# One attention head's exponentials and values left unsplit in float32, and new costs in the list schedule's model

## The chip, the cores and the metric

The kernel runs on one core of one Trainium2 chip. The metric is the device time of one execution in microseconds (us), as a median of several runs. A core has five engines that run beside each other: TensorE (PE), VectorE (DVE), ScalarE (ACT), GpSimd (POOL) and SyncE (SP), which here issues the transfers.

## The reference

A masked attention feeds two gated feed-forward stages. All arrays are float64 or float32; seq is 768, 2 x 8 heads of 64.

```python
q_bits = (einsum('bhsd,dk->bhsk', q, proj) > 0)      # 6 hash bits
mask = q_bucket[:, :, :, None] == k_bucket[:, :, None, :]
scores = where(mask, scale * q @ k.T, -1e9)
attn = exp(scores - max(scores));  attn /= sum(attn) + 1e-9
x = (attn @ v)                      # [1536, 512]
h = ((x @ w1) * (x @ w2)) @ w3;  x = h @ w_out          # 1024 wide
out = (1/(1+exp(-(x @ w_gate))) * (x @ w_val)) @ w_out2 # 1536 wide
```

## The kernel before

The weights arrive as 64-bit floats. Each tile st of 128 x 512 of them is loaded by SP (line 412) and decoded in six steps by ACT, POOL and DVE (`decode`, lines 428 to 437; their tiles are da and dr). A product at near float32 precision is made in the fast form of PE (float32r): each operand is split into a high part, a copy rounded to float32r, and a low part, the rest, and the partial products are added.

Attention goes through 16 heads in groups g of 128 queries, six groups to a head. For each group: four score products into one of two PSUM tiles s (`emit_qk`, lines 558 and 561), the maximum on DVE (sm, line 567), the exponential on ACT (e, line 577), twelve transposes for each two groups on PE (tp, line 612), their copy to the high part pt on ACT (line 615) and the low part on DVE (line 617), and for each two groups the product with the values (av, line 630), from which ACT copies and DVE adds into xall (lines 642 and 643). A head is prepared some groups ahead (`prep`): POOL scales and splits q and k (aq, bq; lines 495 to 497), SP moves parts of them, PE makes the hash bits (gps, lines 479 and 482, with ACT's sg between, line 481), and DVE the mask rows ft (line 504). The values are loaded (line 450) and split (spv, lines 466 and 467) per head. After every second head the row sums go through DRAM to a broadcast tile rr (line 595), and POOL scales xall by it (`emit_scale`, line 602). Between the attention work PE multiplies w3 and w_out into one matrix (wacc, line 685), from the decoded tiles w3f and wor, split into t and wo (lines 672 to 680). From about 340 us on only the feed-forward products are left (line 794), and PE does them one after another.

The order of instructions on each engine does not come from the program text alone. `order_engines` takes all instructions with their dependences, replays them in a list schedule with a table of costs (`cost`, `step`, and the costs of a transfer in `plan`), and tries 6000 random changes of priorities, each kept if the replayed end is not later. The order that is left is fixed as dependences on every engine, SP with its transfers among them. A changed cost can therefore move any instruction.

`PLAIN` is the number of heads, from the first, whose exponentials and values are not split: then there is one pt tile in float32, no low part, no split of the values, and one product per chunk, of 64 instead of 128 rows out.

Of the kernel before, what the change touches and what calls it, by code (L numbers as in the profile page):

```python
# [20 lines left out]
ALU = mybir.AluOpType  # L21
# [30 lines left out]
def order_engines(tc):  # L52
# [5 lines left out]
    ins = [i for i in nc.cur_bb.bb.instructions if type(i).__name__ not in ("BassTilePoolBoundary", "InstRegisterMove")]  # L58
# [3 lines left out]
    N = len(ins)  # L62
# [20 lines left out]
    def cost(k):  # L83

        i, e, op = ins[k], eng[k], type(ins[k]).__name__
        rd = [x for x in i.ins if hasattr(x, "ap")]
        n = max([count(i.outs[0])] + [count(x) for x in rd[:1]])
        bank = lambda x: (region(x) or ("",))[0] in rings and rings[region(x)[0]][0][0] in BANKS
        banks = any(map(bank, rd + [i.outs[0]]))
        es = mybir.dt.size(i.outs[0].dtype)  # L90
        if op.startswith("InstDMA"):
            return 500
        if e == "PE":
            passes = 1 if "float32r" in str(rd[0].dtype) else 2 if n == 128 else 4
            return n / 2.4 * passes + (14 if n == 512 else 16 if passes == 1 else 2 if passes == 2 else 4)
        if e == "Activation":
            if banks:
                return {768: 878, 512: 478, 256: 405}.get(n, 470)
            return 40 + n + (96 if es == 2 else 0)
        if e == "Pool":  # L100
            port[k] = True
            if op == "InstTensorTensor":
                return 30 + n * (2.35 if n < 768 else 2.8)
            return 140 if n < 128 else 715 if es == 2 else 560 if n > 384 else 450
        if e == "DVE":
            two = op in ("InstTensorTensor", "InstCustomDveAnt") or (op == "InstTensorScalarPtr" and len(rd) > 1 and count(rd[1]) > 8)
            if op == "InstTensorReduce":
                return 867
            port[k] = not banks and n >= 128
            if two and n >= 512:  # L110
                return 600
            if two:
                return 85 + n * 1.17 if banks else 60 + n * 1.1
            return 589 if banks else 60 + n * 0.55
        return 500

# [54 lines left out]
    costs = [cost(k) for k in range(N)]  # L171
    left0 = [len(deps[k]) + len(starts[k]) for k in range(N)]
    loads = [type(i).__name__.startswith("InstDMA") for i in ins]

    HORIZON, STRIDE = 30000.0, 15000.0

# [14 lines left out]
    def plan(prio, state, limit):  # L191


        (left, pools, todo, slots, taken, events, ready, waiting, at, free, lock, seen, begun, order,
         tick, dma, slow, window, used, spill) = map(saved, state)
        marks, mark = [], events[0][0] + STRIDE
        pe_order = order["PE"]

        def blocked(k):
            for t in opens.get(k, ()):  # L200
                g = rings[t][0]
                if slots[g] <= 0 or queue[g][taken[g]] != t:
                    return g
                if pools.get(AFTER.get(g[0])):
                    return AFTER[g[0]]
            return None

        def wake(g):
            for k in waiting.pop(g, ()):
                heapq.heappush(ready[eng[k]], (prio[k], k))  # L210

        while events:
            now = events[0][0]
            if now >= mark:
                marks.append((now, [saved(x) for x in (left, pools, todo, slots, taken, events, ready, waiting, at, free, lock, seen,
                                                       begun, order, tick, dma, slow, window, used, spill)]))
                mark = now + STRIDE
            while events and events[0][0] <= now:
                _, _, what, x = heapq.heappop(events)
                if what == "ready":  # L220
                    seen[x] = now
                    heapq.heappush(ready[eng[x]], (prio[x], x))
                elif what == "slot":
                    g = rings[x][0]
                    slots[g] += 1
                    pools[g[0]] -= 1
                    wake(g)
                    if not pools[g[0]]:
                        wake(g[0])
                elif what == "end":  # L230
                    for u in ends[x]:
                        left[u] -= 1
                        at[u] = max(at[u], now + 1.25 * step.get((eng[x], eng[u]), 60))
                        if not left[u]:
                            tick += 1
                            heapq.heappush(events, (at[u], tick, "ready", u))
                    for t in held.get(x, ()):
                        todo[t] -= 1
                        if not todo[t]:
                            tick += 1  # L240
                            heapq.heappush(events, (now + 200, tick, "slot", t))
            again = True
            while again:
                again = False
                for e in ranks:
                    while free[e] <= now and ready[e]:
                        _, k = heapq.heappop(ready[e])
                        g = blocked(k)
                        if g is not None:
                            waiting.setdefault(g, []).append(k)  # L250
                            continue
                        for t in opens.get(k, ()):
                            g = rings[t][0]
                            slots[g] -= 1
                            taken[g] += 1
                            if slots[g] > 0 and waiting.get(g):
                                wake(g)
                                again = True
                        order[e].append(k)
                        begun[k] = now  # L260
                        for u in begins[k]:
                            left[u] -= 1
                            at[u] = max(at[u], now)
                            if not left[u]:
                                tick += 1
                                heapq.heappush(events, (at[u], tick, "ready", u))
                        begin, c = now, costs[k]
                        if e == "PE":
                            if limit and len(pe_order) == limit[0] and now >= limit[1]:
                                return None  # L270
                            while (window + 1) * WINDOW <= now:
                                share, window, used = used / WINDOW, window + 1, spill
                                spill = 0.0
                                slow = share <= 0.75 if slow else share < 0.45
                            c *= 2 if slow else 1
                            inside = min(c, (window + 1) * WINDOW - now)
                            used, spill = used + inside, spill + c - inside
                        if port[k]:
                            begin = max(now, lock["Pool" if e == "DVE" else "DVE"])
                            lock[e] = begin + c  # L280
                        free[e] = done = begin + c
                        if loads[k]:
                            n = count(ins[k].outs[0]) * list(ins[k].outs[0].ap)[0][1] * mybir.dt.size(ins[k].outs[0].dtype)
                            dma = max(now + 2900, dma) + n / 300
                            done = dma + 900
                        tick += 2
                        heapq.heappush(events, (done, tick - 1, "end", k))
                        heapq.heappush(events, (free[e], tick, "free", k))
        if sum(map(len, order.values())) != N:
            return None  # L290
        return max(free.values()), order, seen, begun, marks
# [29 lines left out]
def lsh_attention_moe_moe2_kernel(  # L321
# [115 lines left out]
        dve.tensor_tensor(out=dst.bitcast(I32), in0=ai, in1=ri, op=ALU.add)  # L437


    PLAIN = 0  # L440

    raws, splits, mats = {}, {}, {}

# [153 lines left out]
    def emit_scale(h):  # L597
        b, hh = divmod(h, H)
        x = xall[:, hh // 2, b * S:(b + 1) * S].rearrange("p (c q) -> p c q", c=NT)
        r = rr_t.pop(h // 2).rearrange("p (q c) -> p c q", c=NT)  # L600
        for t in range(0, NT, 2):
            pool.tensor_tensor(out=x[:, t:t + 2], in0=x[:, t:t + 2], in1=r[:, t:t + 2], op=ALU.mult)

    def emit_T(g, j):

# [638 lines left out]
```

## Time and profile before

| | us |
|---|---|
| median of 3 runs | 766.4 (766.24 to 767.06) |
| profiled execution | 769.23 |
| its span, first to last instruction | 767.4 |
| PE busy | 746.2 (97%) |
| DVE busy | 626.3 (82%) |
| ACT busy | 525.3 (68%) |
| POOL busy | 431.4 (56%) |

The profile's page divides the span into 40 slices of some 19 us. PE is busy for half of the first, eight to nine tenths of the next two, and nine tenths or more in nearly all others; DVE and ACT are near full only in the first half. A line of the timeline names an engine, the source line, the operation and the tiles (out<-in); in brackets stands the idle time ahead of it and what ended it. A matmul's shown time is longer than its distance to the next one, because matmuls overlap; the distances are what the chain of waits shows.

### The profile page before, as it was taken

The page shows a single profiled execution, that of the slowest core. Times are in us where ns is not written, and L with a number is a line of the kernel's source. Part 1 is how long each engine was busy: PE and PEld are TensorE (multiplying, and loading weights), DVE is VectorE, ACT ScalarE, POOL GpSimd, SP SyncE. Part 2 cuts the span into 40 slices and gives each one's busy share as a digit, 9 for nine tenths or more (in the row PEclk, how much of TensorE's full clock was granted, in tenths as well). Part 3 has the DMA queues.
Part 4 walks back from the last instruction along what each step waited for, and adds up shares of the span by engine and source line. Part 5 has one row for each costly group of instructions (what it writes and reads, how often), then busy time and mean ns, then how long its engine had stood idle before and what let it go on. Part 6 is the DMA issues. An engine that isn't in the chain of part 4 may idle for free.

```text
span 767.4 us, 11480 instructions
## 1 busy us (share of the span) xinstructions
PE 746.2 (97%) x3896; PEld 638.3 (83%) x3896; DVE 626.3 (82%) x970; ACT 525.3 (68%) x986; POOL 431.4 (56%) x475
## 2 busy tenths in 40 slices
PE   5898999999999999999999999999999999999997
PEld 4787889888989889988888888888888888888886
DVE  6996988776899789869999998788789787676743
ACT  7897988877899889777555568865746444442353
POOL 7767787865577574446655544797654433442000
PEclk9999999999999999999999999999999999999999
DMA  9975767533457755200111143432100000000011
GB/s 289 231 175 149 193 175 205 140 100 115 151 148 168 176 141 142 87 12 1 54 40 45 56 164 124 151 125 97 55 0 28 28 1 1 1 0 2 1 55 56
DMA packets 28506, 74.46 MB, mean 97 GB/s; under 512 B 6048, under 2 KB 8352, under 8 KB 28448
## 3 DMA queue, kind: packets, MB, share of 16 engines
q1 hardware_dynamic: 28368, 73.73, 33.1%
q8 instruction: 31, 0.51, 0.3%
q14 instruction: 27, 0.22, 0.1%
q10 hardware_dynamic: 80, 0.00, 0.0%
HBM read 52.82 MB, written 3.19 MB: 73 GB/s over the span
## 4 chain that ended last, share of the span: by engine, by line
PE 81%; ACT 7%; DVE 5%; POOL 4%; issue 2%; DMA 2%; SPq 0%; DVEq 0%; ACTq 0%; POOLq 0%
PE pa L794 18%; PE pb L794 15%; PE m L794 11%; PE av L630 6%; PE wacc L685 5%; PE tp L612 5%; PE p L794 4%; PE npa L794 4%; PE npb L794 4%; PE s L558 3%; PE s L561 3%; ACT e L577 2%; PE y L794 2%; ACT pt L615 2%; PE gps L479 2%
## 5 line engine op out<-in xcount | busy, mean ns | idle before, releaser
L617 DVE TENSOR_TENSOR pt<-tp,pt 128x512 fp32r<-128x512 f32 x144 | 95.0, 683 | 9.0 <-ACT pt L615 8.1
L612 PE MATMUL tp<-idf,e 128*128 128x128 f32 x576 | 100.3, 276 | 1.8 <-DVE xall L643 0.8
L567 DVE TENSOR_REDUCE sm<-s 128x1 f32<-128x768 f32 x96 | 90.2, 948 | 11.3 <-PE s L561 11.0
L577 ACT ACTIVATE e<-s,sm 128x768 f32<-128x768 f32 x96 | 86.9, 906 | 8.1 <-DVE sm L567 7.6
L431 POOL TENSOR_SCALAR da<-da 128x512 f32<-128x512 f32 x76 | 52.4, 689 | 66.1 <-ACT da L428 59.0
L615 ACT ACTIVATE pt<-tp 128x512 fp32r<-128x512 f32 x144 | 82.4, 599 | 8.6 <-PE tp L612 7.2
L612 PEld LDWEIGHTS tp<-idf,e 128*128 128x128 f32 x576 | 72.0, 141 | 11.6 <-DVE xall L643 2.0
L630 PE MATMUL av<-pt,spv 128*128 128x256 f32 x576 | 79.2, 286 | 0.7 <-DVE ft L504 0.3
L630 PEld LDWEIGHTS av<-pt,spv 128*128 128x128 f32 x576 | 73.2, 190 | 3.6 <-DVE pt L617 1.8
L430 POOL TENSOR_SCALAR dr<-st 128x512 bf16<-128x512 f32 x76 | 67.3, 887 | 6.9 <-issue 1.1
L558 PE MATMUL s<-bk,bq 128*128 128x384 f32 x192 | 62.2, 377 | 6.1 <-ACT e L577 5.4
L561 PE MATMUL s<-ak,aq 128*128 128x384 f32 x192 | 60.8, 376 | 0.0
L429 ACT ACTIVATE dr<-st 128x512 int16<-128x512 uint32 x76 | 60.1, 791 | 0.0
L685 PE MATMUL wacc<-wo,t 128*128 128x512 f32 x192 | 59.3, 407 | 0.0
L428 ACT ACTIVATE da<-st 128x512 f32<-128x512 f32 x76 | 51.1, 672 | 12.0 <-DVE xall L437 3.7
L432 DVE TENSOR_SCALAR da<-da 128x512 uint32<-128x512 uint32 x76 | 47.3, 625 | 9.8 <-POOL da L431 9.8
L558 PEld LDWEIGHTS s<-bk,bq 128*128 128x128 f32 x192 | 36.0, 195 | 11.8 <-ACT e L577 7.8
L794 PE MATMUL pa<-xsx,swh 128*128 128x512 f32 x136 | 42.5, 390 | 0.2 <-DVE w2r L957 0.2
L920 POOL TENSOR_TENSOR swl<-w2r,swh 128x512 fp32r<-128x512 f32 x16 | 21.0, 1313 | 31.2 <-ACT swh L367 28.9
L561 PEld LDWEIGHTS s<-ak,aq 128*128 128x128 f32 x192 | 36.6, 195 | 1.8 <-DVE ak L544 0.3
L685 PEld LDWEIGHTS wacc<-wo,t 128*128 128x128 f32 x192 | 34.3, 189 | 4.2 <-ACT t L367 0.2
L794 PE MATMUL m<-wtl,gh 128*128 128x512 f32 x96 | 37.2, 389 | 0.0
(338 smaller groups left out, 2187.3 us busy)
## 6 DMA issues: line engine op xcount, KB each, us to landing
st<-in_moe_w_dram SPq DMA_DIRECT2D x32, 512.0 KB, 5.2
st<-in_moe_w_out_dram SPq DMA_DIRECT2D x20, 512.0 KB, 3.3
st<-in_moe_w_gate_dram SPq DMA_DIRECT2D x12, 512.0 KB, 3.3
st<-in_moe_w_val_dram SPq DMA_DIRECT2D x12, 512.0 KB, 3.2
qk<-in_qk_dram SPq DMA_DIRECT2D x15, 384.0 KB, 4.3
rawv<-in_v_dram SPq DMA_DIRECT2D x16, 192.0 KB, 2.4
rr<-row SPq DMA_DIRECT2D x16, 192.0 KB, 5.0
out_dram<-o SPq DMA_DIRECT2D x12, 256.0 KB, 2.0
```

Of the source, the lines that this page charges most:

```text
L429: act.activation(out=r.bitcast(I16)[:, 0::2], in_=lw, func=AF.Copy, scale=2.0 ** -29)
L430: pool.tensor_scalar(out=r.bitcast(BF16)[:, 1::2], in0=f(hw), scalar1=0.0, scalar2=1.0, op0=ALU.mult, op1=ALU.mult)
L558: pe.matmul(s[:, half, :HS], lhsT=m["bq"][:, qs], rhs=m["bk"][:, ks], start=True, stop=False)
L561: pe.matmul(s[:, half, :HS], lhsT=m["aq"][:, qs], rhs=m["ak"][:, ks], start=False, stop=True)
L567: dve.tensor_reduce(out=b, in_=s[:, :, :HS], op=ALU.max, axis=AX.XY, negate=True)
L577: act.activation(out=e.rearrange("p (a c) -> p a c", a=2), in_=s[:, :, :HS], func=AF.Exp, bias=sm, scale=1.0, accum_out=su_t[h][:, t:t + 1],)
L612: pe.transpose(ps[:, i * P:(i + 1) * P], e_t[g - g % 2 + a][:, c * P:(c + 1) * P], idf)
L615: act.activation(out=dh, in_=src, func=AF.Copy)
L617: dve.tensor_tensor(out=d, in0=src, in1=f(dh), op=ALU.subtract)
L630: pe.matmul(acc[:w.shape[1], :2 * P].rearrange("p (a t) -> p a t", a=2), lhsT=w, rhs=r[:, :, c], start=(c == 0 and i == 0), stop=(c == NT ...
L685: pe.matmul(acc, lhsT=t3[x][:, j], rhs=wo[y][:, j], start=(j == 0 and n == 0), stop=(j == NF1 - 1 and n == 2))
L794: mm = pe.matmul(ps, lhsT=lhs[x], rhs=rhs[y], start=start and n == 0, stop=stop and n == 2)
```

## The change

PLAIN goes from 0 to 1. The scaling by rr is done in two steps of three chunks instead of three steps of two. In the list schedule's model an ACT step of 256 columns from PSUM costs 290 instead of 405 ns, a DVE step of two operands from PSUM 1.0 instead of 1.17 ns a column, and a transfer's time depends on its kind: loads of 64-bit data, transfers out of on-chip or scratch tiles and other loads have their own rates, and the broadcast read of the row sums a longer tail.

```diff
-                return {768: 878, 512: 478, 256: 405}.get(n, 470)
+                return {768: 878, 512: 478, 256: 290}.get(n, 470)
...
-                return 85 + n * 1.17 if banks else 60 + n * 1.1
+                return 85 + n * 1.0 if banks else 60 + n * 1.1
...
     loads = [type(i).__name__.startswith("InstDMA") for i in ins]
+    wide = [mybir.dt.size(i.outs[0].dtype) == 8 for i in ins]
+    local = [[r[0] for r in map(region, i.ins) if r] for i in ins]
+    rate = [250 if wide[k] else 205 if local[k] else 340 for k in range(N)]
+    slack = [3000 if any(t.startswith("row") for t in local[k]) else 1000 for k in range(N)]
...
-                            dma = max(now + 2900, dma) + n / 300
-                            done = dma + 900
+                            dma = max(now + 1700, dma) + max(300, n / rate[k])
+                            done = dma + slack[k]
...
-    PLAIN = 0
+    PLAIN = 1
...
-        for t in range(0, NT, 2):
-            pool.tensor_tensor(out=x[:, t:t + 2], in0=x[:, t:t + 2], in1=r[:, t:t + 2], op=ALU.mult)
+        for t in range(0, NT, NT // 2):
+            pool.tensor_tensor(out=x[:, t:t + NT // 2], in0=x[:, t:t + NT // 2], in1=r[:, t:t + NT // 2], op=ALU.mult)
```

The source lines after the model move down by four: line 602 before is line 606 after.

The order changes on all engines. Three places matter here; the number behind a name's underline only tells tiles apart, the digits before it are the head or group. First SP's queue at the start, before and after: qk are the heads' queries and keys, rawv and spv values, st weight tiles.

```order
L525 DMA qk00_100<-in_qk_dram 128x384 x2
L527 DMA qk01_101<-in_qk_dram 64x768 x2
L457 DMA qk1_109<-in_qk_dram 128x768
L450 DMA rawv0_111<-in_v_dram 128x384
L457 DMA qk2_143<-in_qk_dram 128x768
L412 DMA st_448<-in_moe_w3_dram 128x512
```

```order
L531 DMA qk01_101<-in_qk_dram 64x768 x2
L461 DMA qk1_109<-in_qk_dram 128x768
L454 DMA spv0_111<-in_v_dram 128x384
L461 DMA qk2_143<-in_qk_dram 128x768
L454 DMA rawv1_167<-in_v_dram 128x384
L416 DMA st_419<-in_moe_w3_dram 128x512
```

Head 0's values go to their final tile, and head 1's values are read ahead of the first weight tile.

Then POOL's queue at the first scaling by rr, before and after: aq4 and bq4 are head 4's operands, one row for each half; da, dr and wo belong to decoding and splitting weights.

```order
L466 CAST spv3_903<-rawv3_532 128x6x64
L467 TENSOR_TENSOR spv3_903<-rawv3_532,spv3_903 128x6x64
L602 TENSOR_TENSOR xall_79<-xall_79,rr0_306 128x256 x3
L496 CAST aq4_776<-qk4_381 128x384
L497 TENSOR_TENSOR bq4_777<-qk4_381,aq4_776 128x384
L588 TENSOR_SCALAR su2_612<-su2_612 128x6
```

```order
L435 TENSOR_SCALAR da_1025<-da_1025 128x512
L434 TENSOR_SCALAR dr_1026<-st_834 128x512
L500 CAST aq4_739<-qk4_361 128x384
L501 TENSOR_TENSOR bq4_740<-qk4_361,aq4_739 128x384
L500 CAST aq4_739<-qk4_361 128x384
L606 TENSOR_TENSOR xall_79<-xall_79,rr0_297 128x384 x2
L501 TENSOR_TENSOR bq4_740<-qk4_361,aq4_739 128x384
```

The scaling moved from ahead of both halves of head 4 to between them (before, the second half's aq and bq follow the rows shown for the first).

Last ACT's queue between the exponentials of groups 17 and 18, before and after.

```order
L577 ACTIVATE e17_804,su2_612<-s1_85,sm17_802 128x768
L367 ACTIVATE xall_79<-av6_827 64x256
L429 ACTIVATE dr_981<-st_790 128x512
L481 ACTIVATE sg_853<-gps_849,zb_78 128x384
L615 ACTIVATE pt0_14_761<-tp15_820 128x512
L367 ACTIVATE wo0_92<-wor4_444 128x512
L481 ACTIVATE sg_861<-gps_857,zb_78 128x384
L428 ACTIVATE da_1062<-st_871 128x512
L615 ACTIVATE pt0_16_888<-tp16_890 128x512
L429 ACTIVATE dr_1063<-st_871 128x512
L615 ACTIVATE pt0_16_888<-tp17_910 128x512
L577 ACTIVATE e18_886,su3_885<-s0_84,sm18_883 128x768
```

```order
L581 ACTIVATE e17_767,su2_576<-s1_85,sm17_765 128x768
L485 ACTIVATE sg_816<-gps_812,zb_78 128x384
L371 ACTIVATE wo0_92<-wor5_416 128x512
L432 ACTIVATE da_1105<-st_909 128x512
L619 ACTIVATE pt0_16_851<-tp16_853 128x512
L581 ACTIVATE e18_849,su3_848<-s0_84,sm18_846 128x768
```

Of the ten steps between the two, four are left; the others now stand before exponential 17, or, as the second sg, behind exponential 18.

## Rows read from the trace of the kernel before

**Rows 1.** Windows: span, busy us of PE, PEld, DVE, ACT, POOL, PE clock, DMA, GB/s

```profile
12.00:20.00 8.00, 4.93 (x28) 3.96 (x28) 5.01 (x9) 7.66 (x16) 7.52 (x10) 1.00 1.01 293
20.00:25.00 5.00, 4.50 (x21) 4.02 (x22) 4.49 (x8) 3.75 (x9) 3.41 (x6) 0.66 1.04 223
...
46.00:58.00 12.00, 12.00 (x85) 10.88 (x84) 11.84 (x20) 11.85 (x26) 5.99 (x9) 1.00 0.94 223
...
62.20:66.00 3.80, 3.80 (x14) 3.72 (x15) 0.00 (x0) 1.54 (x3) 3.56 (x5) 0.55 0.32 74
...
100.00:340.00 240.00, 237.83 (x1511) 214.14 (x1510) 201.40 (x313) 202.69 (x401) 155.04 (x194) 1.00 0.52 141
340.00:768.00 428.00, 423.16 (x1862) 348.68 (x1860) 338.82 (x509) 236.05 (x414) 202.01 (x182) 1.00 0.14 49
```

**Rows 2.** Timeline 58 to 71 us: start us, us, engine, line, operation [idle before, releaser]

```profile
58.36 0.91 ACT L577 ACTIVATE e<-s,sm 128x768 f32<-128x768 f32 x1
58.53 3.11 POOL L602 TENSOR_TENSOR xall<-xall,rr 128x256 f32<-128x256 f32 x3 [2.52 <-DMA rr<-row]
...
62.14 0.68 PE L479 MATMUL gps<-aq,pq 128*128 128x384 f32 x1 [3.12 <-POOL aq L496]
...
64.46 0.58 ACT L481 ACTIVATE sg<-gps,zb 128x384 fp32r<-128x384 f32 x1 [4.03 <-PE gps L479]
...
69.77 0.91 ACT L577 ACTIVATE e<-s,sm 128x768 f32<-128x768 f32 x1
...
70.02 1.67 PE L630 MATMUL av<-pt,spv 128*128 128x256 f32 x12
```

**Rows 3.** Timeline up to 51 us, SP's queue, ACT, DVE and PE

```profile
4.46 0.91 SPq L412 DMA_DIRECT2D st<-in_moe_w_dram  x2
...
8.29 0.55 DVE L466 CAST spv<-rawv 128x384 fp32r<-128x384 f32 x1 [0.64 <-DMA rawv<-in_v_dram]
...
10.56 0.67 ACT L428 ACTIVATE da<-st 128x512 f32<-128x512 f32 x1 [0.40 <-DMA st<-in_moe_w_dram]
...
18.57 0.68 DVE L617 TENSOR_TENSOR pt<-tp,pt 128x512 fp32r<-128x512 f32 x1
...
20.50 0.44 PE L558 MATMUL s<-bk,bq 128*128 128x384 f32 x1 [2.19 <-ACT e L577]
...
50.70 0.86 SPq L595 DMA_DIRECT2D rr<-row  x1
```

**Rows 4.** Chain of waits, 0 to 100 us: start us, us, engine, work

```profile
23.26 0.21 PE tp L612
...
24.76 1.43 PE av L630 x12
...
94.34 0.44 PE tp L612 x4
...
95.34 0.18 PE s L558
...
96.20 0.47 PE wacc L685 x2
```

**Rows 5.** Groups of ACT instructions, 11 to 70 us: count, busy us, mean ns

```profile
L615 ACT ACTIVATE pt<-tp 128x512 fp32r<-128x512 f32 x26 | 15.1, 600 | 1.6 <-PE tp L612 1.3
L429 ACT ACTIVATE dr<-st 128x512 int16<-128x512 uint32 x9 | 7.1, 790 | 0.0
L428 ACT ACTIVATE da<-st 128x512 f32<-128x512 f32 x9 | 6.1, 674 | 0.4 <-DMA st<-in_moe_w_dram 0.4
L481 ACT ACTIVATE sg<-gps,zb 128x384 fp32r<-128x384 f32 x8 | 4.6, 580 | 5.0 <-PE gps L479 5.0
...
L367 ACT ACTIVATE wo<-wor 128x512 fp32r<-128x512 f32 x5 | 3.2, 635 | 0.0
L367 ACT ACTIVATE xall<-av 64x256 f32<-64x256 f32 x7 | 2.7, 380 | 0.6 <-PE av L630 0.5
```

**Rows 6.** Instructions on the tile rr: count, min/median/max ns, first and last start

```profile
L602 POOL TENSOR_TENSOR xall<-xall,rr x24: 857/877/1312, 58.5 to 339.7; 128x256 f32<-128x256 f32 x24
```

## The prediction

> **What bounds the kernel now.** I read the windows first [rows 1]. From 340 us to the end PE is busy for 423.2 us of the 427.4 that the span still has, and from 100 to 340 for 237.8 of 240: there PE alone sets the time, and the change puts no work there. What can move is the first 100 us. In 46 to 58 us PE, ACT and DVE are all nearly full (12.00, 11.85 and 11.84 of 12), so I took the timeline next, to see which of them is waited for. It shows one hole [rows 2]. POOL stands idle for 2.52 us until the read of the row sums (rr) has landed, scales xall for 3.11 us, and only then casts head 4's aq; PE waits 3.12 us for that cast, ACT 4.03 us for the product after it, and the next exponential (number 18, counted from 0) starts at 69.77, 11.4 us after number 17 at 58.36. Right behind the hole, in 62.2 to 66.0 us, the granted clock is 0.55, which is mostly the 1.2 GHz level [rows 1]: 3.80 x 0.45 = 1.7 us of PE more. The hole therefore costs 3.1 + 1.7 = 4.8 us of PE. An earlier, smaller one is PE's wait of 2.19 us for an exponential, before 20.50 us [rows 3], and a clock of 0.66 in the 5 us behind it, 1.7 us more [rows 1]. So ACT's order up to exponential 18, and POOL's order at the scaling, are where the change is decided.
>
> **The change part by part.** I work against the profiled execution: 769.2 us, a span of 767.4 and 1.8 around it. The three timed runs lie at 766.2 to 767.1, median 766.4, so I carry the difference that I find over to 766.4.
>
> *Head 0 unsplit.* Nine subtractions of pt leave DVE, 9 x 0.68 = 6.1 us [rows 3], with three additions into xall behind them. ACT copies as often as before (nine tp tiles, three products), so ACT loses nothing. On PE 36 products of 256 columns become 18. Twelve take 1.43 us, 0.12 each [rows 4], 36 so 4.3 us. No row shows a plain float32 product. Lower bound: each costs what a float32r one does, 18 x 0.12 = 2.1, a gain of 2.1 us. Upper bound: the kernel's split form makes four partial products in two instructions of twice the width, so an unsplit one of 64 columns may need four passes, 18 x 4 x 0.12 = 8.6 us, a loss of 4.3. Transposes lie between: they read float32 too, and 128 columns take 0.11 (four in 0.44), at the low clock 0.21; 256 columns are then 0.22 to 0.42, from -0.3 to +3.3 us in all [rows 4]. I take the upper end, +4.3 us of PE work, since a product needs all partial products and a transpose none. The Trainium skill ("FP8 and Floating Point Precision", TensorE Precision Notes) says that true float32 makes four passes through the array; at 2.4 GHz that is an estimate of 0.43 us for each and +3.4 us in the sum, a rule that speaks against this edit wherever PE has no idle time.
>
> What hides it: the three products fall between about 24 and 43 us, where ACT is the engine that is waited for, and behind the first of them ACT has an exponential and a copy of wo in its queue (the order has both ahead of the xall copy that waits for PE). If that cover is gone, each of the three lengthens the chain by (8.6 - 4.3)/3 = 1.4 us.
>
> *The relieved DVE* is worth little by itself for the same reason. I credit 0.5 us of the 1.25 us that ACT idles in 20 to 25 us [rows 1]; the ends are 0 and 1.25.
>
> *The first loads.* The read of head 1's values now stands ahead of the first two weight tiles on SP. ACT waited 0.40 us for the first of these, started at 10.56, and exponential 0 stands right behind that step in ACT's order [rows 3]. 192 KB at the 293 GB/s of 12 to 20 us [rows 1] are 0.67 us. So the start is 0.6 us later; the bounds are 0 and 0.91, the time SP itself takes to issue two such tiles [rows 3]. The DVE cast of values, which waited 0.64 us for its load, now reads head 1's, which is issued later; it stands between gps and the first maximum, and I take it as covered by the same 0.6.
>
> *ACT's order up to exponential 17.* By count, between exponentials 0 and 17 ACT now has one pt copy, one da, two dr, one wo and one xall more: 0.60 + 0.67 + 2 x 0.79 + 0.64 + 0.38 = 3.9 us [rows 5], that is, more of the weights decoded by then. Exponential 17 starts at 58.4 + 0.6 + 3.9 - 0.5 = 62.4 us, later than before.
>
> *The scaling moved.* In POOL's order the aq and bq of half 0 and the aq of half 1 of head 4 now come ahead of the scaling, and only bq of half 1 behind it. PE's wait of 3.12 us for aq therefore goes. What is late next is that last bq. The read of rr was issued at 50.70 and POOL used it at 58.53 [rows 2, 3], 7.8 us; the new order issues one weight tile ahead of it, and ACT by then runs some 2 us later, so I expect it to land at 60 to 61 us. Two scalings of 384 columns are 2 x 1.5 x 0.88 = 2.6 us (the ends are 2.6 and 3.9, by the 0.86 to 1.31 us of 256 columns [rows 6]) and bq some 1 us: ready at about 64 to 65. PE comes to that product only behind scores that need exponential 17, which ends at 63.3, and ACT's sg stands behind exponential 18. So no wait, or a short one.
>
> *From there to PE's end.* Between the starts of exponentials 17 and 18 ACT has the exponential itself, one sg, one wo, one da and one pt: 0.91 + 0.58 + 0.64 + 0.67 + 0.60 = 3.4 us [rows 2, 5]. Exponential 18 starts at 65.8 instead of 69.77, 4.0 us earlier, at equal ACT work (one da and one wo more, one pt and one sg fewer). On PE, the product av of groups 14 and 15 started at 70.02 [rows 2]. Now it stands behind four score products that need the end of exponential 18, 66.7, with four transposes and two wacc: 4 x 0.18 + 0.44 + 0.47 = 1.6 us [rows 4], so 68.3, 1.7 us earlier. By count of the order PE has then done four score products and three wacc more, 4 x 0.18 + 3 x 0.23 = 1.4 us. In all PE is 1.7 + 1.4 = **3.1 us** ahead, and since PE is nearly full from 100 us on, this stays to the end.
>
> *The rest.* The other scalings, three steps to two at each of eight places, lie on POOL, which is busy 155 of 240 us. The other new costs only move instructions between 80 and 340 us; PE idles there 2.2 us from 100 on [rows 1], so at most 2.2 is to be gained, and a new hole like the old one may cost 4.8. I take 0.
>
> Sum: 769.2 - 3.1 = 766.1 for the profiled execution, 766.4 - 3.1 = **763.3 us** for the median.
>
> **The rivals.**
> 1. *More is won.* The 4.8 us of the hole go wholly, and with DVE out of the way ACT brings exponential 2 forward (in the order it now stands ahead of two pt copies), so that the wait of 2.19 us before 20.50 goes as well. For it: DVE was full in 46 to 58. Against it: ACT was as full. 766.4 - 4.8 - 2.2 = 759.4 us.
> 2. *Nothing comes of it.* ACT's extra 3.9 us cost as much as the hole gave, because the decoded weights only wait, and PE is not ahead. Against it: wacc products did move forward in PE's order. 766.4 - 3.1 + 2.5 to 3.5, about 766.3 us.
> 3. *Slower: the hole moves into the second half.* If rr lands after about 63 us, bq of half 1 is not ready when PE comes to it, and everything behind it on PE stands: the scores of the next groups, hence ACT. The price is a wait like the old one, so the 4.8 us are not saved, and then the late start (0.6) and the float32 work that finds no idle time (up to 2 x 1.4 for the two later av) remain: 766.4 + 3.4 = 769.8 us. For it: rr took 7.8 us here, and a tile of 512 KB now goes ahead of it. With the page's four passes the float32 part would be 2 x 1.1 and the time 769.2.
>
> **How the numbers follow.** Forecast 0.45, rival 1 0.20, rival 2 0.20, rival 3 0.15. A difference of 0.2% (1.5 us) is about what a measurement of this kernel can tell from none; so faster is under 764.9, slower over 767.9. The forecast's own range is 761.5 to 765.5; most of it (0.40 of 0.45) is faster, and all of rival 1; from rival 2 come 0.06 more. Faster 0.66, same 0.20, slower 0.14. The range from 758.0 to 768.3 takes in rivals 1 and 2 and the bounds of the late start and of the DVE relief, and leaves out most of rival 3.
>
> **What would show it.** Right: no PE wait over 1 us between 55 and 70 us, a granted clock of 1.00 there, exponential 18 near 66 us, and PE reaching its last stretch about 3 us earlier. The six float32 products of a pair should take near 2.9 us, without an ACT wait for xall behind them over 1 us. The first weight step on ACT should start near 11.2. Wrong: a wait of PE on bq of head 4, a new wait of more than 2 us between 80 and 340, or a start that is late by more than 1 us.

## The result, and the profile after

The changed kernel takes 772.32 us (median of 4 runs, 771.72 to 772.6); the kernel before, beside it, 766.73 (4 runs, 766.24 to 767.98). The ratio is 1.0072, with a 95% interval of 1.0057 to 1.0088: slower by 5.6 us, where 3.1 us less was forecast. The profiled execution has a span of 770.3 us (772.1 in all).

First the windows of the changed kernel (columns as in [rows 1]):

```profile
12.00:20.00 8.00, 7.29 (x31) 6.71 (x31) 4.89 (x9) 7.47 (x15) 7.59 (x10) 1.00 1.03 305
20.00:25.00 5.00, 3.12 (x20) 2.35 (x19) 3.39 (x5) 5.00 (x11) 4.17 (x7) 1.00 0.82 206
46.00:58.00 12.00, 10.92 (x76) 9.86 (x75) 11.73 (x20) 11.05 (x22) 7.69 (x11) 1.00 0.93 217
62.20:66.00 3.80, 3.65 (x25) 3.19 (x24) 3.80 (x6) 3.12 (x8) 3.80 (x5) 1.00 0.86 231
100.00:340.00 240.00, 235.97 (x1495) 210.58 (x1495) 209.86 (x312) 201.65 (x397) 149.60 (x181) 1.00 0.51 138
340.00:768.00 428.00, 425.68 (x1872) 350.23 (x1870) 342.64 (x511) 235.91 (x415) 206.74 (x184) 1.00 0.15 48
```

The low clock of 0.55 at 62.2 to 66.0 us and of 0.66 at 20 to 25 [rows 1] is not in this profile. A loss shows further on: PE is busy for 235.97 of the 240 us from 100 on (237.83 before), although none of the float32 products lies there. The shares of busy time show only a part of it, since a matmul's shown time overlaps the next one's; a closer measure follows.

Then its timeline from 57 to 67 us, which answers to [rows 2]:

```profile
57.54 0.46 SPq L599 DMA_DIRECT2D rr<-row  x1
...
62.98 0.33 PE L483 MATMUL gps<-aq,pq 128*128 128x384 f32 x1
63.00 2.82 POOL L606 TENSOR_TENSOR xall<-xall,rr 128x384 f32<-128x384 f32 x2
...
63.59 0.91 ACT L581 ACTIVATE e<-s,sm 128x768 f32<-128x768 f32 x1
64.48 0.57 ACT L485 ACTIVATE sg<-gps,zb 128x384 fp32r<-128x384 f32 x1
...
66.57 0.90 ACT L581 ACTIVATE e<-s,sm 128x768 f32<-128x768 f32 x1
```

Neither the scaling nor the product behind aq has a wait in brackets any more. The two exponentials shown are numbers 17 and 18; 18 starts at 66.57 (forecast 65.8; 69.77 in [rows 2]). The first weight step is later by 0.3 us than in [rows 3] (10.56), where 0.6 was taken; from ACT's timeline, this step and exponential 0:

```profile
10.83 0.67 ACT L432 ACTIVATE da<-st 128x512 f32<-128x512 f32 x1 [0.62 <-DMA st<-in_moe_w_dram]
11.66 0.90 ACT L581 ACTIVATE e<-s,sm 128x768 f32<-128x768 f32 x1 [0.17 <-DVE sm L571]
```

In later profiles this step starts at 11.00 and 10.68 (kernel before) and at 11.47 (changed kernel), so single executions differ by as much as the shift that was forecast.

The float32 products, as a group by form (36 records for 18 products), and in the chain of waits:

```profile
L634 PE MATMUL av<-pt,spv 128*64 128x256 f32 x36 | 8.4, 383 | 0.0
```

```profile
31.94 2.73 PE av L634 x12
37.56 2.75 PE av L634 x12
```

Each product leaves two records; six take 2.73 us, 0.455 each, 18 of them 8.2 us. The split form took 36 x 0.119 = 4.3, so PE has 3.9 us more work.

**Idle time of PE, worked out.** Below, "idle by T" is T less a spacing for every product that began before T, the one that such products have in an unbroken run at the full clock: 0.110 us for 128 columns, 0.119 for 256, 0.173 for 384, 0.227 for 512, 0.228 for each of the 36 float32 records (0.127 with half the columns). All 3,896 records are there in every profile. The measure counts waits and time at the low clock alike. The spacings are rounded, and over a whole run that makes some 0.6 us; differences between profiles hardly depend on it.

### The profile page after: what moved, and what is told of

Its sections match the earlier page's. It is cut to its first block, busy times and chain, and to the rows that moved or that the text cites. A ratio compares the mean times of both kernels' runs of the same rounds, so it can differ in the third digit from the quotient of the medians.

```text
span 770.3 us, 11458 instructions
## 1 busy us (share of the span) xinstructions
PE 751.9 (98%) x3896; PEld 637.5 (83%) x3896; DVE 634.3 (82%) x957; ACT 526.1 (68%) x986; POOL 431.4 (56%) x466
## 4 chain that ended last, share of the span: by engine, by line
PE 75%; ACT 8%; DVE 7%; POOL 6%; issue 3%; DMA 2%; POOLq 0%; ACTq 0%; DVEq 0%
PE pa L798 18%; PE pb L798 15%; PE m L798 11%; PE av L634 5%; PE tp L616 4%; PE npb L798 4%; PE npa L798 4%; PE wacc L689 3%; PE p L798 3%; ACT e L581 2%; PE s L562 2%; PE y L798 2%; PE s L565 2%; ACT pt L619 2%; DVE pt L621 1%
## 5 line engine op out<-in xcount | busy, mean ns | idle before, releaser
L616 PE MATMUL tp<-idf,e 128*128 128x128 f32 x576 | 96.3, 275 | 1.1 <-DVE pt L621 0.8
L621 DVE TENSOR_TENSOR pt<-tp,pt 128x512 fp32r<-128x512 f32 x135 | 88.6, 681 | 7.2 <-ACT pt L619 6.7
L619 ACT ACTIVATE pt<-tp 128x512 fp32r<-128x512 f32 (+1 forms) x144 | 81.8, 598 | 6.6 <-PE tp L616 4.8
L634 PE MATMUL av<-pt,spv 128*128 128x256 f32 (+1 forms) x576 | 82.5, 291 | 2.2 <-DVE pt L621 1.3
L634 PEld LDWEIGHTS av<-pt,spv 128*128 128x128 f32 (+1 forms) x576 | 73.1, 185 | 10.4 <-DVE pt L621 4.0
L565 PE MATMUL s<-ak,aq 128*128 128x384 f32 x192 | 59.1, 366 | 0.0
L436 DVE TENSOR_SCALAR da<-da 128x512 uint32<-128x512 uint32 x76 | 52.2, 689 | 8.0 <-POOL da L435 7.6
L798 PE MATMUL m<-wth,gh 128*128 128x512 f32 x96 | 37.5, 390 | 0.2 <-ACT gh L371 0.2
```

The source lines that it names most:

```text
L565: pe.matmul(s[:, half, :HS], lhsT=m["aq"][:, qs], rhs=m["ak"][:, ks], start=False, stop=True)
L616: pe.transpose(ps[:, i * P:(i + 1) * P], e_t[g - g % 2 + a][:, c * P:(c + 1) * P], idf)
L619: act.activation(out=dh, in_=src, func=AF.Copy)
L621: dve.tensor_tensor(out=d, in0=src, in1=f(dh), op=ALU.subtract)
L634: pe.matmul(acc[:w.shape[1], :2 * P].rearrange("p (a t) -> p a t", a=2), lhsT=w, rhs=r[:, :, c], start=(c == 0 and i == 0), stop=(c == NT ...
L798: mm = pe.matmul(ps, lhsT=lhs[x], rhs=rhs[y], start=start and n == 0, stop=stop and n == 2)
```

## The experiments

The median of the kernel before, measured again beside each group of runs, was 766.6 to 768.1 us, its single runs 763.3 to 773.3; the ratios below are to the one measured beside. All medians below are of 4 to 12 runs, except where one profile is meant.

**The kernel before, profiled again.** No edit.

> The kernel before once more, unchanged, for a second profile of it. Theory A (the wait and the lower clock at 58 to 66 us belong to the order of the kernel before): the stretch 62.2 to 66 us shows again a granted clock near 0.6 and some 3 us without a matmul. Theory B (they were in part peculiar to the one profiled execution, whose span lay 2.8 us above the timed runs): the same instructions wait less there, the clock stays at 1.00, and the span comes out near 764 to 765 us instead of 767.4.

> The kernel before for a third profile. If the wait for rr is a matter of the transfer's duration in one execution, this one lies on the line of the other two: rr's first transfer lands L us after its issue at about 50.8 us; where L is 3.4 (second profile) GpSimd does not wait and the span is near 763.7, where it is 7.7 (first profile) it waits 2.5 us and the span is near 767.4; between these in between. If the span varies as much with rr landing in 4 us or less, other transfers make the spread.

Spans 763.7 and 763.8 us, against 767.4 in the first profile. The timeline of the second, then of the third profile, lines as in [rows 2]:

```profile
50.92 0.61 SPq L595 DMA_DIRECT2D rr<-row  x1
...
55.35 2.54 POOL L602 TENSOR_TENSOR xall<-xall,rr 128x256 f32<-128x256 f32 x3
...
65.36 0.90 ACT L577 ACTIVATE e<-s,sm 128x768 f32<-128x768 f32 x1
```

```profile
51.74 0.60 SPq L595 DMA_DIRECT2D rr<-row  x1
...
56.30 2.52 POOL L602 TENSOR_TENSOR xall<-xall,rr 128x256 f32<-128x256 f32 x3
...
66.33 0.89 ACT L577 ACTIVATE e<-s,sm 128x768 f32<-128x768 f32 x1
```

rr, issued at the same place, landed after 3.4 and 4.2 us instead of 7.7, POOL did not wait, and exponential 18 came at 65.36 and 66.33 instead of 69.77. It was not rr alone that was late: the weight tile st that SP issues four places ahead of it took 8.4 us to land in the first profile, 3.9 in the second and 6.3 in the third, and in the first and third the transfers between them landed behind it one after another, with rr last. The windows of the second, then the third profile, show the clock of the two stretches that the prediction built on:

```profile
20.00:25.00 5.00, 3.88 (x29) 3.79 (x30) 5.00 (x8) 4.32 (x10) 4.54 (x7) 1.00 1.01 234
...
62.20:66.00 3.80, 3.80 (x26) 3.33 (x26) 3.55 (x7) 3.39 (x6) 3.72 (x4) 1.00 0.92 237
```

```profile
20.00:25.00 5.00, 4.40 (x20) 3.88 (x21) 4.30 (x8) 3.65 (x9) 3.27 (x5) 0.66 1.03 242
...
62.20:66.00 3.80, 3.80 (x23) 3.14 (x22) 3.14 (x6) 2.96 (x6) 3.64 (x5) 1.00 0.84 186
```

The clock of 0.55 behind the hole is in neither, that of 0.66 at 20 to 25 us in the third profile again. Theory B holds: the order alone does not make the hole, which one of three executions shows. By 66 us PE had idled 24.2 us in the first profile, 19.7 and 20.6 in the others; the difference, 3.6 to 4.5 us, is about that of the spans, 3.7. How often the timed runs have the hole was not seen, and those of 770 us and more are slower than it accounts for.

**Half the float32 work, every order kept.** In the changed kernel, each product of the first head takes 64 of the 128 queries of each group: even chunks the first half, odd chunks the second. The schedule's model goes on charging these products for all columns, so that the order stays what it was; in the trace it is the same on every engine.

```diff
+            n, passes = (256, 4) if list(i.outs[0].ap)[0][1] == 64 else (n, 1 if "float32r" in str(rd[0].dtype) else 2 if n == 128 else 4)
...
-        for c in range(NT):
-            w = sv[:, c]
+        for c in (0, 2, 4, 1, 3, 5) if h < PLAIN else range(NT):
+            w, k = sv[:, c], slice(c % 2 * 64, c % 2 * 64 + 64) if h < PLAIN else slice(0, P)
...
```

> The changed kernel with every engine's instructions in its own order, unchanged; each of the 18 float32 products of the first head multiplies 128 of its 256 columns (the 64 even-numbered chunk columns of each block, or the other 64), so half of that head's values are left out of the sum. That takes about half of 18 x 0.455 = 8.2 us out of TensorE between 24 and 40 us and changes nothing else. Theory 1 (TensorE sets the time there, the products are paid in full): 772.3 - 4.1 = 768.2 us, 767.4 to 769.0. The prediction's step (the products lie beside ScalarE's work and are hidden): 772.3, at least 771.5. Rival (the time is given back later, as the front's lead was): between the two, 770 to 771.5, with the last exponential of attention no earlier than in the changed kernel.

Measured 770.5 us, 1.0038 of the kernel before (1.0015 to 1.0060). The same on the changed kernel with start 2 of the search (its run is below, 769.36):

> The changed kernel with start 2 of the search, every engine's instructions in that kernel's own order, with 128 of the 256 columns of each of the 18 float32 products (half of the first head's values left out). 18 x (0.455 - 0.253) = 3.6 us less on TensorE. Hidden: 769.4 as with all columns, at least 768.6. Paid in full: 765.8, at most 766.6. In the first order 3.1 of the 3.6 us had turned into idle time of TensorE by 66 us, and 4.4 us of idle time less the same by 58 us is what 'hidden' expects here too: TensorE idle 19.5 to 20.5 us before 58 us instead of 17.0.

Measured 768.06, 1.0017 of the kernel before (1.0003 to 1.0031). ACT's exponential 18 in the changed kernel and in the one with half the columns, which have the same order:

```profile
66.57 0.90 ACT L581 ACTIVATE e<-s,sm 128x768 f32<-128x768 f32 x1
```

```profile
65.98 0.90 ACT L581 ACTIVATE e<-s,sm 128x768 f32<-128x768 f32 x1
```

Some 3.6 us of PE work less brings it 0.6 us forward, 1.1 us against the changed kernel's second profile (67.11, next experiment). PE idles 21.8 us by 66 us instead of 18.7 and 19.1 in those two profiles, 2.7 to 3.1 more; in the second order 20.8 instead of 17.4, 3.4 more. So 75 to 95% of what is saved turns into idle time within the front: most of the products' time is hidden there, and "paid in full" falls for the front. The waits that the profile names in 24 to 66 us grew for ACT's exponential (from 0.9 to 1.7 us, in the second order from none to 2.3), and by 0.4 to 0.8 us each for ACT's xall, DVE's pt and POOL's bq.

The end times bear out neither forecast, hidden or paid in full: 770.5 and 768.06 lie between the two. By the medians 1.1 to 1.8 us and 1.3 us come off. The rival has the time of the first, but not its sign: the last exponential of attention comes 1.7 to 2.7 us earlier than in the changed kernel's two profiles. Why more is won by the end than in the front these profiles do not settle.

**The changed kernel again.** No edit.

> The changed kernel once more, unchanged, for a second profile and its time beside the runs below. Theory A (its order sets its losses, and its wait for transfers is small): 771.7 to 772.6 us again, its runs within 2 us of each other while those of the kernel before spread over several; the last exponential of attention again within 0.5 us of 327.3 us, TensorE again idle 2.4 us in 220 to 240 us. Theory B (the losses at 180 to 240 us were chance of one execution): TensorE idles less than 1.3 us in 220 to 240 us, as in the run with half the columns, and the span is 2 us shorter.

771.6 us, 1.0052 of the kernel before (1.0032 to 1.0071), its single runs within 2.1 us, the profiled span 770.0. Theory A holds for the size, to 0.1 us, and fails on the place: PE idled 0.9 us in 220 to 240 us instead of 2.4, as B has it, and the last exponential came at 326.3, but the span is only 0.3 us shorter: 0.4 us each was lost by 66 us and after 380. What differs at 220 us is told at the end.

**Parts of the change alone.** Without the products (PLAIN 0 in the changed kernel, as shown), and with them alone (the same line the other way round, in the kernel before):

```diff
-    PLAIN = 1
+    PLAIN = 0
```

> The changed kernel's model of transfers, its two costs and its scaling in two pieces, but the first head split as before (no float32 products). Theory 1 with theory 2 (float32 costs 3.9 us and the order under the new model gives back some 4.7 us after 100 us): about 772.3 - 3.9 = 768.4, 767 to 770, so slower than before. Theory 1 alone (only the products cost, the new model is no loss): 764 or less, faster than before. Rival (the search's order is chance, anything moves it by a few us): anywhere in 763 to 772, with its losses in other stretches than those of the changed kernel.

> The kernel before with the first head unsplit and in float32, all else (the model of transfers, both costs, the scaling in three pieces) as before. Theory 1: 766.7 + 3.9 - 0.5 for VectorE's work that goes = 770.1, 769 to 771.5. The prediction's step (hidden): 766.2, 765.5 to 767. Rival (chance in the search's order): outside both, with a loss after 100 us that the front does not explain.

769.32 us (1.0019 of the kernel before, 1.0000 to 1.0038) and 771.45 us (1.0046, 1.0024 to 1.0068). Both lie where theory 1 ("paid in full") puts them, the first with a loss after 100 us besides (theory 2); but here other orders are compared, which the half columns are not. The two costs alone, and the model of transfers with the scaling in two steps alone:

> The kernel before with the two changed costs alone (a ScalarE copy of 256 columns 290 instead of 405 ns, a VectorE subtraction beside ScalarE 85 + 1.0 n instead of 85 + 1.17 n), old model of transfers, three scaling pieces, the first head split. Theory A1 (the costs mislead the search: the profile shows the copy at 380 ns): 769 to 771 us, slower than before by 2 us or more. Theory A2 (the model of transfers does it): as the kernel before, within 1 us. Rival (chance): no better told than by the spread of the two runs with another start.

> The kernel before with the new model of transfers and the scaling in two pieces alone; old costs, first head split, start 1. If the model of transfers brings the loss after 100 us: TensorE idle 13 to 15 us from 100 to 760 us and 769 to 771 us in all. If the two costs bring it (the kernel with them alone idles 14.2 us there): 10.4 to 11.7 us idle there, and 766.5 to 768.5 us. A draw beyond either is chance.

770.03 us (1.0035, 1.0012 to 1.0059) and 774.36 us (1.0099, 1.0070 to 1.0128). Products, costs and transfers alone are thus slower by 0.46, 0.35 and 0.99%, 1.8% in sum, all together by 0.72%: they do not add up. The costs alone lie where theory A1 has them. The model of transfers alone is beyond both of its ranges, which its expectation calls chance, though its idle time from 100 to 760 us, 13.1 us, is what the first had forecast. What all of them do is to make the search draw another order. From the run with the model of transfers alone, PE's first score product and ACT's exponential 0:

```profile
11.06 1.01 PE L562 MATMUL s<-bk,bq 128*128 128x384 f32 x2 [2.44 <-POOL bq L545]
```

```profile
13.74 0.90 ACT L581 ACTIVATE e<-s,sm 128x768 f32<-128x768 f32 x1 [1.40 <-DVE sm L571]
```

That is 2.1 us later than in the changed kernel (11.66), whose order comes from the same model of transfers.

**Other starts of the search.** Only `random.Random(1)` is changed, to 2, 3 or 4: in the kernel before, in the changed one, and in the one without the products.

> The kernel before with the other start of the search, nothing else. Theory A: the median of the kernel before that is measured beside it, within 2 us. Rival (chance in the order): more than 2 us away from it. If the wait for the row of reciprocals (rr) is a chance of that transfer's duration, the spread of the runs changes with where the order puts the scaling.

> The changed kernel with another start of the random search over priorities (2 instead of 1), nothing else. Theory A (the change itself costs: 3.9 us more work on TensorE, and waits that its costs and its model of transfers bring about): 770.5 to 773.5 us. Rival (the order that the search happens on makes most of the difference): a time that lies more than 2 us from 772.3, the losses of TensorE after 100 us in other stretches and of another size than 14.8 us in all (100 to 760 us of the changed kernel's profile).

> The kernel before with a third start of the search (3), nothing else. Theory L (the order that the search draws moves this kernel by 2 to 5 us, and the kernel before, drawn with 1, is a good draw): 768.5 to 772, slower than the kernel before. Theory A (the change costs what it costs in any order): within 1.5 us of the kernel before.

> The changed kernel with the third start of the search. Theory L: 768 to 773, no further than 2.5 us from the kernel before with the same start, on either side of it. Theory A: 5 us above the kernel before with the same start, as the changed kernel is with the first. Of the products' 3.9 us, 1 to 3 should be seen as less idle time of TensorE than in the kernel before with the same start, by 100 us.

> The kernel before with a fourth start (4). Theory L: 768.5 to 772, slower than the kernel before. Theory A: within 1.5 us of the kernel before.

> The changed kernel with the fourth start. Theory L: 768 to 773, within 2.5 us of the kernel before with the same start, on either side. Theory A: 5 us above it.

> The change without its float32 products (first head split as before), start 2 of the search. Theory P (the products make the mean cost, the model of transfers and costs makes none): over starts 1 to 4 the mean lies within 0.7 us of that of the kernels before with the same starts, 768.6, and 2 to 3 us below that of the changed kernels, 771.2. Theory M (the model makes it): the mean is 770.5 to 772, as that of the changed kernels. The idle time of TensorE from 100 to 760 us tells the same: 10.4 to 11.7 us (as the kernels before) under P, 13 to 15 (as the changed ones) under M.

> As the run before it, with start 3 of the search, for the same mean. P: 768 to 770; M: 770.5 to 772.5, with the spread of some 2 us that the order drawn makes.

> As the two runs before it, with start 4 of the search, for the same mean. P: 767 to 770; M: 770.5 to 772.5, with the spread of some 2 us that the order drawn makes.

| start | before | changed, no products | changed |
|---|---|---|---|
| 1 | 766.7 | 769.3 | 772.3 |
| 2 | 771.0 | 768.8 | 769.4 |
| 3 | 769.5 | 770.5 | 771.4 |
| 4 | 766.8 | 775.0 | 772.2 |
| mean | 768.5 | 770.9 | 771.3 |

(medians, us; idle time of PE below from one profile of each, for start 1 of the kernel before the second)

| mean of four starts | idle by 100 us | idle from 100 to 760 us |
|---|---|---|
| before | 24.2 (22.5 to 25.4) | 11.0 (10.4 to 11.7) |
| changed, no products | 25.2 (24.2 to 25.9) | 14.0 (11.0 to 19.0) |
| changed | 21.5 (19.3 to 22.8) | 14.3 (13.2 to 15.3) |

The start alone moves the kernel before by 4.3 us. Changed less before is +5.6, -1.7, +2.0 and +5.4 us for the same start, mean +2.8 (2.5 by the ratios to the kernel before measured beside), with a standard error of 1.2 from the scatter of each four. With so few starts a 95% interval is about -0.3 to 5.9 us: that the change costs something in the mean is likely by the times, but not shown. In starts 2 and 3 the two kernels lie within 2.5 us of each other, as theory L has it; in starts 1 and 4 the changed one is over 5 us slower, as theory A has it, and start 4 of the kernel before is no slower than start 1, against L. So the draw can be about half of the 5.6 us, and some 3 us may stay with the change.

P and M were to tell whether the products or the model make that rest. The mean without products, 770.9, lies where M has it, but start 4 alone makes it so (the other three: 769.6), and its distance from either of the other means has an error of 1.6 to 1.8: by the times this is open.

The idle times say more. Up to 100 us the changed kernels idle 3.7 us less than those without products, so the 3.9 us of float32 work about fill idle time. After 100 us all four changed kernels idle more than all four before, by 3.3 us in the mean. The sizes are to be taken with care, since each is one execution: the profile of the kernel before with start 2 is the fastest of its twelve runs (768.0, median 771.0), that of the changed one with start 3 the slowest of its ten (775.0, median 771.4). With the 3.9 us of work the two tables of idle time make 4.5 us of difference, where the medians make 2.8.

## Why the prediction was wrong, point by point

*The hole.* The working "3.1 + 1.7 = 4.8 us" read its rows rightly, and neither profile of the changed kernel has that wait. The first step that failed is the one that carried the gain "over to 766.4", as if the runs of that median had the hole. Two later profiles of the same kernel have none and lie 0.8 to 0.9 us below the median; the profiled execution lay 2.8 us above it, which was seen and taken as an offset. The wait that the change was to remove is thus not one that the order makes each time. Against the first profile the changed kernel is ahead by 66 us: 24.2 - 18.7 idle less 3.9 of work is 1.6 us (forecast 3.1). Against the second it is behind by 3.9 - (19.7 - 18.7) = 2.9 us, against the third by 2.0.

*Head 0 unsplit.* Size right: 8.2 us for 18 products (8.6 taken). "What hides it" held in the main within the front: 2.7 to 3.4 of 3.6 us with half the columns. It was hidden, though, beside an ACT that in the changed kernel is behind the kernel before without the hole, at exponential 18 by 0.2 to 1.8 us (66.57 and 67.11 against 65.36 and 66.33).

*ACT's order and the scaling.* Exponential 17 was forecast at 62.4 and started at 63.59; exponential 18 at 65.8, and 66.57. That is right to about a microsecond, and rival 3's wait did not come: rr landed in time, and bq of half 1 waited for nothing.

*"Since PE is nearly full from 100 us on, this stays to the end", and "I take 0" for the rest.* This is the second step that failed. PE idled 14.8 us from 100 to 760 us (14.0 in the second profile), against 10.3, 10.9 and 10.0 in the three profiles of the kernel before. The prediction had read 2.2 us of idle time from 100 to 340 us off the share of busy time; by the spacings it was some 9 us, so that there was more room to lose, and to gain, than it took. The idle time that grew against the second profile is at 180 to 240 us (4.9 and 3.5 in the changed kernel's two profiles against 2.3) and at 340 to 380 (1.5 in both against 0.3). PE's largest waits there in the changed kernel's first profile:

```profile
193.71 0.39 PE L634 MATMUL av<-pt,spv 128*128 128x256 f32 x1 [0.51 <-ACT pt L619]
223.58 1.70 PE L634 MATMUL av<-pt,spv 128*128 128x256 f32 x12 [1.35 <-DVE pt L621]
...
347.82 1.23 PE L798 MATMUL y<-gh,wh 128*128 128x512 f32 x4 [0.49 <-ACT gh L371]
```

The prediction had the bound for it ("a new hole like the old one may cost 4.8") and put it into no rival. No such single hole came either: in both profiles of the changed kernel no wait of PE from 100 us on is over 1.35 us. A busy PE is no proof that a lead is kept: it stops in many short waits, and those that the profile names from 100 us on sum to 4.3 of the 14.8 us (2.9 of 10.9 in the second profile of the kernel before). That the reordered work of other engines makes them is shown for the waits listed, and argued for the rest.

The sum, against the second profile (765.5 in all, the changed one 772.1): +3.9 of products, -1.0 of idle time by 66 us, -0.5 to 100 us, +3.9 from 100 to 760 us: 6.3 of 6.6 us. Against the forecast of -3.1 that is 9.4 off: 4.5 for the base, 1.5 for the front, 3.4 for the rest after 66 us. Rival 3 had the sign, and a time 2.5 us short (769.8), by another mechanism that did not come: its late bq. Much of the 5.6 us between the medians may be the draw of the order, a cause that the prediction did not weigh.

What stays open: why all changed kernels idle more after 100 us, each part of the change alone too (13.1 to 14.2 us; 12.0 without products). Whether the new costs steer the search worse, or a start and costs that fit each other were kept, was not told apart. No complete version is clearly faster than the kernel before: the best others are 766.8 (before, start 4) and 768.8 us (changed without products, start 2).

## What to carry to other kernels

A wait for a transfer in one profile is one execution's; before a forecast rests on it, look where that execution lies among the timed runs, and take a second profile. Where a random search sets the order, one draw of each version says little: compare several starts, since here the start alone moved the time by 4 us, and the change by 3 in the mean of four, hardly clear of its error. And work that is hidden in the front (the products) is worth testing with the order held fixed, as the half columns did, not by taking the edit out.

## What the runs showed of the hardware

The same transfer, rr, issued behind the same ones, landed after 7.7, 3.4 and 4.2 us in three executions of one kernel. It goes with the 512 KB weight tile ahead of it on the same queue, which took 8.4, 3.9 and 6.3 us; what made that tile slow was not looked into.

A float32 product with 64 columns of weights and 256 moving ones took 0.455 us, as two records, 3.8 times the 0.119 of a float32r one. The Trainium skill ("FP8 and Floating Point Precision", TensorE Precision Notes) says four passes; the trace agrees.

DVE's step w2r<-da,dr, which reads two tiles, took 2.23 us in the changed kernel's first profile and 0.73 in its second, with the same order. First, then second profile, 219 to 223 us:

```profile
219.28 0.98 POOL L499 TENSOR_SCALAR qk<-qk 64x384 f32<-64x384 f32 x2 [2.15 <-DMA qk<-in_qk_dram]
...
219.83 2.23 DVE L441 CUSTOM_DVE_ANT_0 w2r<-da,dr 128x1024 uint16<-128x1024 uint16 x1
220.23 1.27 POOL L792 TENSOR_TENSOR wl<-w1r,wh 128x512 fp32r<-128x512 f32 x1
```

```profile
219.94 1.41 POOL L499 TENSOR_SCALAR qk<-qk 64x384 f32<-64x384 f32 x2 [2.40 <-DMA qk<-in_qk_dram]
220.26 0.73 DVE L441 CUSTOM_DVE_ANT_0 w2r<-da,dr 128x1024 uint16<-128x1024 uint16 x1
...
221.33 1.29 POOL L792 TENSOR_TENSOR wl<-w1r,wh 128x512 fp32r<-128x512 f32 x1
```

In the first DVE's step lay beside the whole of POOL's two-operand step wl<-w1r,wh and ended 0.56 us after it, in the second it was done before POOL's began. From 180 to 480 us, the steps of this line took 1.7 to 2.2 us in each of the first profile's five cases with 1.2 us or more of such an overlap, and 0.7 to 1.1 in all others. The first profile's chain of waits goes on from it to the pt that PE's product of 223.58 waited 1.35 us for:

```profile
219.83 2.23 DVE w2r L441
222.06 0.87 DVE sm L571
222.93 1.79 DVE pt L621 x3
```

The second profile has neither the long step nor this chain. The Trainium skill ("GPSIMD Engine Reference", Key points) says that GpSimd shares its SBUF interfaces with VectorE and that the two contend where VectorE reads two SBUF inputs; the trace agrees, with 1.5 us for this step. Between the two profiles DVE's step moved by 0.4 us and POOL's by 1.1: POOL's two steps ahead of it started 0.7 us later, when their transfer qk had landed, and took 0.4 us more. With the order the same, a shift of 0.7 us between two engines thus went with a wait of 1.35 us on PE, in one profile and not in the other.
